# Turning three of eight blocks of z by a transposing DMA at their reload instead of on TensorE

## The chip, the cores and the metric

The kernel runs on one core of a Trainium2 chip, as one launch. The metric is the device time in microseconds (us). The engines are TensorE (PE), VectorE (DVE), ScalarE (ACT), GpSimd (POOL) and the DMA queues, which are fed here by SyncE (SP) and by POOL. On-chip memory has 128 partitions of SBUF and eight PSUM banks of 2 KB per partition.

## The reference

```python
mod = (silu(c) @ w_mod).reshape(1, 6, 1, 1024)
sa, ca, ga, sb, cb, gb = (mod[:, i] for i in range(6))
h = layernorm(x) * (1 + ca) + sa                    # x: 1 x 2048 x 1024
x = x + ga * (Cre @ (h @ Dre.T) - Cim @ (h @ Dim.T))  # DFT over hidden, then over sequence
h = layernorm(x) * (1 + cb) + sb
y = layernorm(h)
x = x + gb * (gelu(y @ w1 + b1) @ w2 + b2)          # w1: 1024 x 3584, w2: 3584 x 1024
```

All inputs and the output are 32-bit floats.

## The kernel before

**Arithmetic.** Every matrix product is made from 16-bit floats: an operand is split into a high half (the value rounded to 16 bits) and a low half (what is left), and three products high x high, high x low and low x high are added in PSUM (`PASSES`). Products are also blocked in the manner of Strassen and Winograd: two by two blocks need seven products instead of eight, so operands come as seven combinations `m` in the order `ORDER = (0, 1, 2, 4, 3, 6, 5)`, and results are added up from seven PSUM results. `right_tasks` makes the seven combinations of a right operand: its `hi` is an ACT copy to 16 bits (L386), its `comb` a DVE addition (L411), its `lo` a DVE subtraction (L396 without a scale, L398 with one).

**Stages.** First the modulation rows and the layer norm of x. Then the product over the sequence (`plain1`, `winograd1`, L1112 and L1162), whose result u goes through DRAM. Then the second product (`gemm2`, L1394), in eight blocks b of 256 rows: row r of 128 partitions takes pairs of tokens, `PIECES` lists its 14 pieces of 12 matmuls, each with a load of u (`load_up`, L1346). After block b come its residual, both layer norms and the modulation (`ln_tasks(b)`), in which 32-bit rows of z are left in `wb(b)` (two halves of 128 x 1024, written by the ACT instruction at L1279). `load_xw(b)` loads block b's x into the same place, of which there are two, so it waits for block b - 2 to be out of the way.

**The turn.** The MLP needs z with the hidden dimension on the partitions. `turn(b, n)` turns half n of block b: eight transposes of 128 x 128 on PE (`turn_tile`, L1296) into two PSUM banks, then an ACT copy to `zt(b, n)` (L1306). The function `turns`, called after each piece of `gemm2`, places them when the planner has the rows written: block k is turned in block k + 2 of `gemm2`, block 6 in part after its end and in part after the first pass of the MLP, block 7 after the third (`turn_late`, L1864). `z_tasks(b)` then splits the turned block into its seven combinations, high and low, and stores them with POOL's queue to DRAM (`zc_d`, L1328): four blocks to a half h of the tokens, h = 0 for blocks 0 to 3 and h = 1 for 4 to 7.

**The MLP.** `gemm3(g)` (L1585) makes 256 of the 3584 hidden units for half of the tokens: seven products of 12 matmuls, with w1 as the stationary operand and `zc(m)` in SBUF as the moving one. g = 0 to 13 take the first half of the tokens, 14 to 27 the second. Its results go through L1607 (ACT), L1611 (DVE) and L1604 (ACT, the gelu) and are split by `hid_tasks`. `gemm4(v)` (L1694) is the product with w2 and adds into `acc` (L1730, L1740). The order on PE is written out: gemm3(0), then for every v gemm3(2v+1), gemm3(2v+2), gemm4(v).

**The reload.** `zc(m)`, 1 MB each, is held once. The first half is loaded during the eighth block of `gemm2`, as the weights of the DFT in the same places come free. The second half is loaded during gemm3(13): after each of its products the hook `reload(m)` issues `load_zc(1, m)` on SP (L1336), and gemm3(14), which follows directly on PE, uses it one pass later.

**Order.** Work of DVE, ACT, POOL and the DMA queues is put into streams of tasks. A planner, which runs while the program is written and not on the chip, keeps a clock for each engine and picks from the streams by due time, estimated start and cost; what it picks becomes the fixed order of that engine's or queue's instructions. While `gemm2` is planned, DMAs are taken in the order of their estimated starts. `need(tag)` takes all tasks with a tag before going on. SP's queue is in order: an issue that waits for a semaphore holds up those behind it.

Of the kernel before, what the change touches and what calls it, by code (L numbers as in the profile page):

```python
# [10 lines left out]
F16 = mybir.dt.float16  # L11
# [6 lines left out]
P = 128  # L18
S = 2048
D = 1024  # L20
# [2 lines left out]
ND = D // P  # L23
TB = 512
NTB = S // TB
EPS = 1e-5


# [7 lines left out]
def kernel(ctx, tc, x, cre, cim, dre, dim, w1, b1, w2, b2, c, wm, out):  # L36
# [117 lines left out]
    O_K, O_ACC, O_HID = 32, 48, 172  # L154

    def zc(m):
        return at(O_ZC[m], 4096, F16).rearrange("p (a k c t) -> p a k c t", a=2, k=4, c=4)

    w1c = at(0, 14336, F16).rearrange("p (m s a x) -> p m s a x", m=7, s=2, a=2)
    w2c = at(144, 14336, F16).rearrange("p (m s a x) -> p m s a x", m=7, s=2, a=2)  # L160
# [13 lines left out]
    def quad(g):  # L174
# [2 lines left out]
    gb2_t = at(28, 1024)  # L177

    zc_d = [
        [dram.tile([P, 2, 4, 4, P], F16, tag=f"zc_{h}_{m}", name=f"zc_{h}_{m}") for m in range(7)] for h in range(2)  # L180
    ]
    s_d = {m: dram.tile([P, 8, 2, 512], F16, tag=f"s_{m}", name=f"s_{m}") for m in (2, 4, 3, 5)}
    u_d = [
        [[dram.tile([P, 2, 4, 2, P], F16, tag=f"u_{t}_{m}_{r}", name=f"u_{t}_{m}_{r}") for r in range(2)] for m in range(7)]
# [873 lines left out]


    PASSES = ((0, 0), (0, 1), (1, 0))  # L1060
    NB = NS // 2
    PIECES = [(m, ri) for m in ORDER for ri in range(2)]
    NP = len(PIECES)

# [139 lines left out]
    def ln_tasks(b):  # L1204

        y, w, cl = yb(b), wb(b), lns[b % 2]
        su, nm, v, ve, r, a = (cl[:, n, :] for n in range(6))
        junk = at(180, 1024, F16)

        def norm(src, scale):  # L1210
            def square(n):
# [64 lines left out]
        t.append(Task("dve", 0.16, lambda: dve.tensor_tensor(nm, nm, r, op=ALU.mult), [t[-1].key]))  # L1276
        k = t[-1].key
        for n in (1, 0):
            f = lambda n=n: act.activation(w[:, n], w[:, n], AF.Identity, scale=r[:, n : n + 1], bias=nm[:, n : n + 1])  # L1279
            t.append(Task("act", 1.25, f, [k], ("w", b, n)))  # L1280
        if b < NB - 1:
            n = len(two_)
# [5 lines left out]
        return t  # L1288

    def zt(b, n):  # L1290
        return at((O_K if b == NB - 1 else 144) + 4 * n, 1024)

    def turn_tile(b, n, ps):

# [3 lines left out]
    def turn(b, n):  # L1298
# [7 lines left out]
        f = lambda: act.activation(zt(b, n), ps, AF.Copy)  # L1306
        push("turn", f"turn{b}", [Task("act", 1.1, f, [("turn", b, n)], ("zt", b, n))], clk["pe"])

    def z_tasks(b):

        e, o = zt(b, 0), zt(b, 1)
        q = [e[:, 0:512], o[:, 0:512], e[:, 512:1024], o[:, 512:1024]]
        places = [O_K + 8 + 2 * k for k in range(4)] if b == NB - 1 else [152, 154, 46 if b == NB - 2 else 182, 216, 218]
        h, k = divmod(b, 4)
        n, at_ = [0], {}

        def outs(m):
            at_[m] = n[0]
            reuse("z", (b, n[0] - len(places)) if n[0] >= len(places) else None)
            if n[0] < len(places) and 0 < b < NB - 1:  # L1320
                need(f"z{b - 1}")
            v = at(places[n[0] % len(places)], 1024, F16).rearrange("p (a x) -> p a x", a=2)
            n[0] += 1
            return v[:, 0], v[:, 1], v

        def post(m, o_):
            dst = zc_d[h][m][:, :, k].rearrange("p a c t -> p a (c t)")
            store("z", (b, at_[m]), lambda: gp.dma_start(dst, o_[2]), ("z", b, m), f"z{b}")  # L1328

        return right_tasks(  # L1330
            q, outs, None, 512, lambda j: ("zt", b, j % 2), lambda m: ("z", b, m), post=post,
            free=lambda m: slot("z", lambda: (b, n[0] - len(places))),
        )

    def load_zc(h, m):
        sp.dma_start(at(O_ZC[m], 4096, F16), zc_d[h][m].rearrange("p a k c t -> p (a k c t)"))  # L1336

    def load_up(N):
        b, n = divmod(N, NP)
# [25 lines left out]
    def load_xw(b):  # L1365
        def f():
            need("st_u")
            sp.dma_start(wb(b), x[2 * b : 2 * b + 2].rearrange("r p e -> p r e"))

        was = [("turn", b - 2, n) for n in range(2)] if b > 1 else [("g1", opn(3, 5, 3))]  # L1370
        if b == 1:
            was += [("uw", 3, ri, m) for ri in range(2) for m in range(7)]
        return Task("dma", 3.0, f, was, ("xw", b))
# [150 lines left out]
        f = lambda q: lambda: sp.dma_start(raw2(0, q), w2[0:2, :, q, :].rearrange("j p x -> p j x"))  # L1524
        return [Task("dma", 1.5, f(q), [("w1", 2 - q // 2, m) for m in range(7)], ("raw2", 0, q)) for q in (2, 3, 0, 1)]

    waiting = deque((k, r) for k in range(NB - 1) for r in (1, 0))
    waiting.pop()

    def turns(b, n):  # L1530

        k, r = waiting[0] if waiting else (NB, 0)
        if k >= b:
            return
        last = NP - 1 if b == NB - 1 else 6 + 3 * (1 - r)
        keys = [("w", k, r)] + ([("zt", *((k, 1) if r == 0 else (k - 1, 0)))] if (k, r) != (0, 1) else [])
        zs = [("z", k - 1, m) for m in range(7)] if k and r else []
        while True:
            k, r = waiting[0]
            late = b == NB - 1 and n == NP - 1 or k < b - 1 and n >= last  # L1540
            if not late and any(done.get(x, 1e12) > clk["pe"] - 0.5 for x in keys + zs):
                return
            waiting.popleft()
            if r:
                need(f"z{k - 1}")
            turn(k, r)
            if r == 0:
                push("z", f"z{k}", z_tasks(k), clk["pe"] + 10.0)
            if not waiting or not late:
                return  # L1550

    def each(b):
        def f(n):
            turns(b, n)

            if n == 1 and 1 <= b < 4:
                push("wl", "wl", first_w1(b - 1))
                push("w", "w", w1_norm(b - 1) + w1_tasks(b - 1), clk["pe"] + 20.0)
            if n == 1 and b == 4:
                push("wl", "wl", first_w2())  # L1560
                push("w", "w", w2_norm(0) + w2_tasks(0), clk["pe"] + 60.0)
            if b == NB - 1:
                if n == 3:
                    need("w", "st_w1", *(f"z{k}" for k in range(4)))
                    for m in ORDER:
                        sp.dma_start(w1c[:, m, 0], w1_d[0][:, m])
                        done["w1", 0, m] = clk["pe"]
                if 4 <= n < 11:
                    load_zc(0, ORDER[n - 4])
                    m = ORDER[n - 4]  # L1570
                    sp.dma_start(w1c[:, m, 1], w1_d[1][:, m])
                    done["w1", 1, m] = clk["pe"]

        return f

    for b in range(NB):
        gemm2(b, each(b))
        push("ln", "ln", ln_tasks(b), clk["pe"] + 10.0)
    need("y")
    in_order[0] = False  # L1580

    def product3(ps, s, m, start):
        for d in range(4):
            for n, (a, b) in enumerate(PASSES):
                pe.matmul(  # L1585
                    ps.rearrange("p (k t) -> p k t", k=4),
                    w1c[:, m, s, a, d * P : (d + 1) * P],
                    zc(m)[:, b, :, d, :],
                    start=(start and d == 0 and n == 0),
                    stop=(d == 3 and n == 2),  # L1590
                    skip_group_check=not start,
                )
# [264 lines left out]

        return f

    def turn_late(b, n):  # L1860
        k, two = take(2)
        turn_tile(b, n, two)
        done["turn", b, n] = clk["pe"]
        act.activation(zt(b, n), two, AF.Copy)  # L1864
        done["zt", b, n] = clk["pe"] + 2.0
        leave(k, 2, clk["pe"] + 2.0)

    later[0] = True
    for j, k in enumerate((3, 4, 5, 6, 7, 1, 2, 0)):
        done["bank", k] = level() - 8.0 + j  # L1870
# [1 line left out]
    for kind, k in seq:  # L1872
        if kind == 3:
# [4 lines left out]
            if g == 0:  # L1878
# [1 line left out]
                    f = lambda m=m: sp.dma_start(w1c[:, m, 0], w1_d[2][:, m])  # L1880
                    Task("dma", 0.75, f, key=("w1", 2, m)).run()
                load_w1(3, *range(4))
                turn_late(NB - 2, 0)
                push("z", f"z{NB - 2}", z_tasks(NB - 2), due[3, 1] + 5)
                push("hid", "hid0", hid_tasks(0), due[3, 1] + 0)
            elif g == 1:
                need(f"z{NB - 2}", "ln", "st_w2", "st_x2")
                load_w1(4, 0, 1)
                for m in ORDER:
                    f = lambda m=m: sp.dma_start(w2c[:, m], w2_d[0][:, m])  # L1890
                    Task("dma", 1.5, f, key=("w2", 0, m)).run()
                push("hid", "hid1", hid_tasks(1), due[4, 0])
                push("w1", "n1_3", w1_norm(3), due[3, 3] - 20.0)
                push_w1(3)
            elif g == 2:
                turn_late(NB - 1, 1)
                turn_late(NB - 1, 0)
                push("z", f"z{NB - 1}", z_tasks(NB - 1), due[4, 0] + 10)
                push_w1(4)

                def f(q):
                    def load():
                        need(f"z{NB - 1}")
                        sp.dma_start(raw2(1, q), w2[2:4, :, q, :].rearrange("j p x -> p j x"))

                    return load

                was = [("z", NB - 1, m) for m in range(7)]
                push("w2", "l2_1", [Task("dma", 1.5, f(q), was, ("raw2", 1, q)) for q in range(4)], due[4, 1] - 20.0)
                push("w2", "n2_1", w2_norm(1), due[4, 1] - 20.0)  # L1910
            else:
                if g == 15:
                    need("fin")
                if g == 2 * NPAIR - 1:
                    push("hid", "hid27b", ht[0][:5], due[4, g // 2] - 20)
                    push("hid", "hid27c", ht[0][5:], due[4, g // 2] + 5)
                elif g % 2 == 1:
                    push("hid", f"hid{g}", hid_tasks(g), due[4, g // 2])
                push_w1(g + 2)
# [61 lines left out]
```

## Time and profile before

| | |
|---|---|
| median of 3 runs | 1991.37 us (1990.52 to 1992.13) |
| the profiled execution, first to last instruction (its span) | 1990.4 us |
| PE busy | 1969.1 us, 99% |
| DVE, ACT, POOL busy | 1417.3, 851.1, 190.5 us |
| mean granted TensorE clock | 0.999 |
| DMA traffic | 402.42 MB, mean 202 GB/s |
| PE transposes (L1296) | 128, 273 ns each, from 733.4 to 1021.1 us |
| stores of z (L1328) | 56 of 256 KB, 4.5 us to landing |
| loads of zc (L1336) | 14 of 1024 KB, 6.9 us to landing |

The profile is one execution seen by the hardware profiler; times in it are us from the span's start, durations of single instructions are ns. "Idle before" is the time for which an engine stood before an instruction, and the arrow names what ended it. SPq and POOLq are the queues that issue DMAs. Matmuls overlap: the row of a matmul lasts 379 ns, while consecutive ones start 216 ns apart.

### The profile page before, as it was taken

Reading aid. Unit: us, or ns where it says so; the run is one execution under the profiler, and the core shown is the slowest. Engines: PE = TensorE matmul, PEld = TensorE weight load, DVE = VectorE, ACT = ScalarE, POOL = GpSimd, SP = SyncE. Lnnn points to the kernel's source line nnn. Section 1 sums busy time; section 2 is a strip of 40 time slices with the busy share of each in tenths; the row PEclk is TensorE's granted clock in tenths of the full one; section 3 lists DMA queues with packets and bytes.
Section 4 is the critical chain, followed back from the end, with each engine's and each line's share of the span. In section 5 each row is a group of like instructions: output and inputs, shape, how many; then the busy total and the mean of one; then the engine's idle time right before and its main releaser. Section 6 shows DMA issues by size and latency. Waiting matters only on the chain. (4 is left out here: it accounts for less than half of the span.)

```text
span 1990.4 us, 23735 instructions
## 1 busy us (share of the span) xinstructions
PE 1969.1 (99%) x9082; PEld 896.5 (45%) x9082; DVE 1417.3 (71%) x1795; ACT 851.1 (43%) x1091; POOL 190.5 (10%) x282
## 2 busy tenths in 40 slices
PE   9999999999999999999999999999999999999999
PEld 3444444444444444444444444444444444444443
DVE  2977886997984467777588999999873353553566
ACT  2853432344542245554477566466233322312311
POOL 0002212221220112221020000000000000000000
PEclk9999999999999999999999999999999999999999
DMA  9138677678779777877765454453477332432323
GB/s 380 53 97 281 236 264 275 246 298 329 249 256 364 271 261 256 282 244 277 276 218 190 171 199 168 145 175 146 169 231 216 117 97 83 127 101 69 111 74 85
DMA packets 139363, 402.42 MB, mean 202 GB/s; under 512 B 15536, under 2 KB 15536, under 8 KB 134640
## 3 DMA queue, kind: packets, MB, share of 16 engines
q1 hardware_dynamic: 112528, 309.92, 45.3%
q0 software_dynamic: 26720, 90.98, 12.8%
q8 instruction: 71, 1.16, 0.2%
q14 instruction: 44, 0.36, 0.1%
HBM read 262.95 MB, written 137.89 MB: 201 GB/s over the span
## 5 line engine op out<-in xcount | busy, mean ns | idle before, releaser
L1694 PE MATMUL ps<-arena 128*128 128x512 f16 x2352 | 511.1, 379 | 2.8 <-DVE arena L1740 1.5
L1585 PE MATMUL ps<-arena 128*128 128x512 f16 x2352 | 510.2, 379 | 2.2 <-ACT arena L1607 2.2
L1162 PE MATMUL ps<-arena 128*128 128x512 f16 x2016 | 435.5, 379 | 1.4 <-DMA arena<-s 1.4
L1694 PEld LDWEIGHTS <-arena 128*128 128x128 f16 x2352 | 229.9, 98 | 281.5 <-issue 3.8
L1585 PEld LDWEIGHTS <-arena 128*128 128x128 f16 x2352 | 230.1, 98 | 279.4 <-issue 2.5
L1740 DVE SCALAR_TENSOR_TENSOR arena<-ps,i4c,arena 128x1024 f32<-128x1024 f32 x179 | 229.3, 1281 | 144.4 <-PE ps L1694 143.1
L1162 PEld LDWEIGHTS <-arena 128*128 128x128 f16 x2016 | 197.1, 98 | 239.5 <-DMA arena<-s 1.9
L1394 PE MATMUL ps<-arena 128*128 128x512 f16 x1344 | 292.4, 379 | 1.9 <-DMA arena<-u 1.9
L386 ACT ACTIVATE arena<-arena,shc 128x512 f16<-128x512 f32 (+1 forms) x115 | 115.9, 1018 | 277.3 <-PE ps L1694 184.6
L1394 PEld LDWEIGHTS <-arena 128*128 128x128 f16 x1344 | 131.4, 98 | 158.0 <-DMA arena<-u 2.4
L1112 PE MATMUL ps<-arena 128*128 128x512 f16 x768 | 167.4, 379 | 7.2 <-ACT arena L635 2.0
L411 DVE TENSOR_TENSOR arena<-arena 128x512 f32<-128x512 f32 (+1 forms) x228 | 171.0, 753 | 4.1
L681 ACT ACTIVATE arena<-arena 128x1024 f16<-128x1024 f32 x100 | 104.1, 1050 | 150.8 <-PE ps L1162 111.4
L398 DVE SCALAR_TENSOR_TENSOR arena<-arena,shc 128x512 f16<-128x512 f32 (+1 forms) x115 | 128.7, 1122 | 38.4 <-ACT arena L386 38.3
L684 DVE SCALAR_TENSOR_TENSOR arena<-arena 128x1024 f16<-128x1024 f32 x100 | 128.6, 1303 | 18.5 <-ACT arena L681 18.5
L1611 DVE TENSOR_TENSOR arena<-arena,ps 128x512 f32<-128x512 f32 x84 | 57.5, 685 | 110.7 <-PE ps L1585 106.5
L1604 ACT ACTIVATE arena<-arena,b1s,i1c 128x512 f32<-128x512 f32 x84 | 68.3, 813 | 137.0 <-DVE arena L1611 137.0
L1112 PEld LDWEIGHTS <-arena 128*128 128x128 f16 x768 | 74.7, 98 | 99.9 <-ACT arena L635 4.0
L773 ACT ACTIVATE arena<-arena 128x1024 f16<-128x1024 f32 x56 | 57.7, 1047 | 60.9 <-DVE arena L1186 18.8
L776 DVE TENSOR_TENSOR arena<-arena 128x1024 f16<-128x1024 f32 x56 | 66.9, 1218 | 14.6 <-ACT arena L773 14.6
L386 ACT ACTIVATE arena<-arena,s1c 128x512 f16<-128x512 f32 (+1 forms) x70 | 60.8, 884 | 36.9 <-DVE arena L411 25.9
L398 DVE SCALAR_TENSOR_TENSOR arena<-arena,s1c 128x512 f16<-128x512 f32 (+1 forms) x70 | 66.3, 959 | 11.0 <-ACT arena L386 10.8
(159 smaller groups left out, 1418.8 us busy)
## 6 DMA issues: line engine op xcount, KB each, us to landing
w<-arena SPq DMA_DIRECT2D x64, 512.0 KB, 5.0
arena<-w SPq DMA_DIRECT2D x119, 256.0 KB, 2.7
u<-arena POOLq DMA_DIRECT2D x56, 512.0 KB, 5.5
arena<-u SPq DMA_DIRECT2D x112, 256.0 KB, 4.0
arena<-w SPq DMA_DIRECT2D x56, 512.0 KB, 3.4
arena<-s SPq DMA_DIRECT2D x48, 512.0 KB, 7.6
arena<-in_cre_dram SPq DMA_DIRECT2D x32, 512.0 KB, 7.3
arena<-in_cim_dram SPq DMA_DIRECT2D x32, 512.0 KB, 5.2
```

Source lines behind the costliest of these rows:

```text
L386: act.activation(o[m][0], q(j), AF.Copy, **sc)
L398: dve.scalar_tensor_tensor(o[m][1], q(j), scale, o[m][0], op0=ALU.mult, op1=ALU.subtract)
L411: dve.tensor_tensor(q(d), q(a), q(b), op=op)
L681: h = Task("act", 1.15, lambda: act.activation(o[:, :, 0], s2, AF.Copy, scale=SC), list(deps) + free)
L684: dve.scalar_tensor_tensor(o[:, :, 1], s2, SC, o[:, :, 0], op0=ALU.mult, op1=ALU.subtract)
L1112: pe.matmul(bank_of(d_), hleft(d_, s, kp, a), cop(n)[:, s, b], start=(kp == 0 and s == 0 and a == 0 and b == 0), stop=(kp == 7 and s == 1 ...
L1162: pe.matmul(bank_of(st + ch), left, cop(n)[:, s, b], start=(start and kp == 0 and s == 0 and a == 0 and b == 0), stop=(kp == 3 and s == 1 ...
L1394: pe.matmul(bank_of(bk), up(N)[:, c_, a], dp(n)[:, c_, w], start=(start and ri == 0 and c_ == 0 and i == 0), stop=(ri == 1 and c_ == 3 and ...
L1585: pe.matmul(ps.rearrange("p (k t) -> p k t", k=4), w1c[:, m, s, a, d * P : (d + 1) * P], zc(m)[:, b, :, d, :], start=(start and d == 0 and ...
L1604: act.activation(dst, src, AF.Gelu_apprx_tanh, scale=inv, bias=b1s[:, 2 * p + j : 2 * p + j + 1])
L1694: pe.matmul(t[:, j], hidc[:, c_, m, a, k * P : (k + 1) * P], w2c[:, m, c_, w], start=(start and c_ == 0 and n == 0), stop=(c_ == 1 and n = ...
L1740: lambda: dve.scalar_tensor_tensor(dst, ps[b], inv, dst, op0=ALU.mult, op1=ALU.add), kp[b],
```

## The change

Blocks 0 to 4 are turned on PE as before (`TURNED = 5`). Blocks 5, 6 and 7 aren't: `z_tasks` splits their rows as they stand, token on the partition, and stores the seven combinations to new tensors `zl_d[m]` (128 x 3 x 1024, 16 bits). `load_zc(1, m)` becomes two DMAs on SP: a transposing one of 128 x 3072 elements from `zl_d[m]`, 24 blocks of 128 x 128, and a plain one of block 4's 128 x 1024. For that the layout of `zc` becomes block by block, so that the stores of z write one run of 2 KB per partition in place of two of 1 KB. `turn_late` and its four calls go; the split of blocks 5 and 6 is pushed during `gemm2`, once blocks 0 to 4 are turned (`later_z`), and the split of block 7 where its turns stood. `load_xw(7)` waits for the splits of block 5, which now read `wb(5)`. Block 7's rows are written to `O_K` (`zw`), and some scratch places move.

```diff
@@ constants
+NB = NS // 2
+TURNED = 5
@@ places and DRAM tensors
     def zc(m):
-        return at(O_ZC[m], 4096, F16).rearrange("p (a k c t) -> p a k c t", a=2, k=4, c=4)
+        return at(O_ZC[m], 4096, F16).rearrange("p (k a c t) -> p k a c t", k=4, a=2, c=4)
...
     zc_d = [
-        [dram.tile([P, 2, 4, 4, P], F16, tag=f"zc_{h}_{m}", name=f"zc_{h}_{m}") for m in range(7)] for h in range(2)
+        [dram.tile([P, 4 * (1 - h) + (TURNED - 4) * h, D], F16, tag=f"zc_{h}_{m}", name=f"zc_{h}_{m}") for m in range(7)]
+        for h in range(2)
     ]
+    zl_d = [dram.tile([P, NB - TURNED, D], F16, tag=f"zl_{m}", name=f"zl_{m}") for m in range(7)]
@@ ln_tasks
-        junk = at(180, 1024, F16)
+        junk = at(O_K + 8 if b == NB - 1 else 180, 1024, F16)
...
-            f = lambda n=n: act.activation(w[:, n], w[:, n], AF.Identity, scale=r[:, n : n + 1], bias=nm[:, n : n + 1])
+            f = lambda n=n: act.activation(zw(b)[:, n], w[:, n], AF.Identity, scale=r[:, n : n + 1], bias=nm[:, n : n + 1])
@@ zt, zw and z_tasks
     def zt(b, n):
-        return at((O_K if b == NB - 1 else 144) + 4 * n, 1024)
+        return at(144 + 4 * n, 1024)
...
+    def zw(b):
+        return at(O_K, 2048).rearrange("p (r e) -> p r e", r=2) if b == NB - 1 else wb(b)
...
-        e, o = zt(b, 0), zt(b, 1)
+        e, o = (zw(b)[:, n] if b >= TURNED else zt(b, n) for n in range(2))
+        src = "w" if b >= TURNED else "zt"
...
-        places = [O_K + 8 + 2 * k for k in range(4)] if b == NB - 1 else [152, 154, 46 if b == NB - 2 else 182, 216, 218]
+        if b < TURNED:
+            places = [152, 154, 182, 216, 218]
+        else:
+            places = [O_K + 8 + 2 * k for k in range(4)] if b == NB - 1 else [144 + 2 * k for k in range(6)]
...
-            dst = zc_d[h][m][:, :, k].rearrange("p a c t -> p a (c t)")
-            store("z", (b, at_[m]), lambda: gp.dma_start(dst, o_[2]), ("z", b, m), f"z{b}")
+            dst = zc_d[h][m][:, k] if b < TURNED else zl_d[m][:, b - TURNED]
+            v = o_[2].rearrange("p a x -> p (a x)")
+            store("z", (b, at_[m]), lambda: gp.dma_start(dst, v), ("z", b, m), f"z{b}")
...
-            q, outs, None, 512, lambda j: ("zt", b, j % 2), lambda m: ("z", b, m), post=post,
+            q, outs, None, 512, lambda j: (src, b, j % 2), lambda m: ("z", b, m), post=post,
@@ load_zc
-        sp.dma_start(at(O_ZC[m], 4096, F16), zc_d[h][m].rearrange("p a k c t -> p (a k c t)"))
+        n = 4 if h == 0 else TURNED - 4
+        o = at(O_ZC[m], 4096, F16)
+        if h:
+            v = o[:, n * D :].rearrange("p (n t) -> p n t", t=P)
+            sp.dma_start_transpose(v, zl_d[m].rearrange("p k x -> p (k x)"))
+        if n:
+            sp.dma_start(o[:, 0 : n * D], zc_d[h][m].rearrange("p k x -> p (k x)"))
@@ load_xw
-        was = [("turn", b - 2, n) for n in range(2)] if b > 1 else [("g1", opn(3, 5, 3))]
+        was = [("g1", opn(3, 5, 3))]
+        if b > 1:
+            was = [("turn", b - 2, n) for n in range(2)] if b - 2 < TURNED else [("z", b - 2, m) for m in range(7)]
@@ turns during gemm2
-    waiting = deque((k, r) for k in range(NB - 1) for r in (1, 0))
-    waiting.pop()
+    waiting = deque((k, r) for k in range(TURNED) for r in (1, 0))
+    later_z = deque()
...
-        last = NP - 1 if b == NB - 1 else 6 + 3 * (1 - r)
+        last = 6 + 3 * (1 - r)
...
-            late = b == NB - 1 and n == NP - 1 or k < b - 1 and n >= last
+            late = k < b - 1 and n >= last
...
             turns(b, n)
+            while later_z and not waiting:
+                k, t = later_z.popleft()
+                push("z", f"z{k}", z_tasks(k), t)
...
         gemm2(b, each(b))
-        push("ln", "ln", ln_tasks(b), clk["pe"] + 10.0)
+        push("ln", f"ln{b}", ln_tasks(b), clk["pe"] + 10.0)
+        if TURNED <= b < NB - 1:
+            later_z.append((b, clk["pe"] + 40.0))
@@ product3
-                    zc(m)[:, b, :, d, :],
+                    zc(m)[:, :, b, d, :],
@@ the order of the MLP (turn_late removed)
-                turn_late(NB - 2, 0)
-                push("z", f"z{NB - 2}", z_tasks(NB - 2), due[3, 1] + 5)
+                need(f"ln{NB - 2}")
                 push("hid", "hid0", hid_tasks(0), due[3, 1] + 0)
             elif g == 1:
-                need(f"z{NB - 2}", "ln", "st_w2", "st_x2")
+                need(f"z{NB - 2}", f"ln{NB - 1}", "st_w2", "st_x2")
...
             elif g == 2:
-                turn_late(NB - 1, 1)
-                turn_late(NB - 1, 0)
                 push("z", f"z{NB - 1}", z_tasks(NB - 1), due[4, 0] + 10)
```

More of the change, by code (lines that the diff above doesn't have):

```diff
@@ L1060 @@
     PASSES = ((0, 0), (0, 1), (1, 0))
-    NB = NS // 2
     PIECES = [(m, ri) for m in ORDER for ri in range(2)]
@@ L1858, in hook @@
         return f
[L1860 to L1866, printed above, removed]
     later[0] = True
```

## The prediction

> **What bounds the kernel now.** I read the page's head first, then the waits of TensorE (PE), then the timeline of PE around the removed instructions.
>
> ```profile
> span 1990.4 us, 23735 instructions
> PE 1969.1 (99%) x9082; PEld 896.5 (45%) x9082; DVE 1417.3 (71%) x1795; ACT 851.1 (43%) x1091; POOL 190.5 (10%) x282
> ...
> PE ps L1585 <- ACT arena L1607: 2.2, 1, 2.2
> ...
> PE ps L1394 <- DMA arena<-u: 1.9, 1, 1.9
> ```
>
> PE is busy 1969.1 of 1990.4 us, and its waits are a handful of single events. Nothing else is near: VectorE (DVE) 71%, ScalarE (ACT) 43%. So an instruction taken off PE shortens the run by the time by which it moves the next matmul, as long as nothing new makes PE wait. Two of the waits lie in the region that the change rearranges. The rows of PE there (start, length, engine and line, operation, count, idle before and what ended it):
>
> ```profile
> 926.06 1.04 PE L1296 MATMUL ps<-ident,arena 128*128 128x128 f32 x8
> 926.94 5.34 PE L1394 MATMUL ps<-arena 128*128 128x512 f16 x24
> 932.12 1.04 PE L1296 MATMUL ps<-ident,arena 128*128 128x128 f32 x8
> 932.99 23.47 PE L1394 MATMUL ps<-arena 128*128 128x512 f16 x108
> 958.38 2.76 PE L1394 MATMUL ps<-arena 128*128 128x512 f16 x12 [1.92 <-DMA arena<-u]
> 960.98 1.04 PE L1296 MATMUL ps<-ident,arena 128*128 128x128 f32 x8
> 961.86 18.29 PE L1585 MATMUL ps<-arena 128*128 128x512 f16 x84
> 979.99 1.04 PE L1296 MATMUL ps<-ident,arena 128*128 128x128 f32 x8
> 980.86 23.47 PE L1585 MATMUL ps<-arena 128*128 128x512 f16 x108
> 1006.54 13.11 PE L1585 MATMUL ps<-arena 128*128 128x512 f16 x60 [2.21 <-ACT arena L1607]
> 1019.49 1.91 PE L1296 MATMUL ps<-ident,arena 128*128 128x128 f32 x16
> 1021.23 5.34 PE L1694 MATMUL ps<-arena 128*128 128x512 f16 x24
> ```
>
> The L1296 rows are the turns of blocks 5, 6 and 7: six halves of eight transposes.
>
> **Part 1, the turns leave PE: -5.2 us.** What a turn costs the path is the distance from its start to the next matmul's start, since matmuls overlap. 926.94-926.06 = 0.88, 932.99-932.12 = 0.87, 961.86-960.98 = 0.88, 980.86-979.99 = 0.87, and 1021.23-1019.49 = 1.74 for the last two: 5.24 us for 48 transposes, 0.109 us each, and no idle time in front of any of them. All of it is on the path. The duration in the row below, 0.273 us, would give 13.1, but it covers pipeline time in which neighbours run.
>
> ```profile
> L1296 PE MATMUL ps<-ident,arena x128: 272/273/273, 733.4 to 1021.1; 128*128 128x128 f32 x128
> L1306 ACT ACTIVATE arena<-ps x13: 1023/1023/1024, 734.5 to 962.1; 128x1024 f32<-128x1024 f32 x13
> ```
>
> The Trainium skill (TensorE: Matmul & The Clock Gate, Part 4: PE-mode transpose) gives about 275 ns for a transpose in one kernel's context; the row's 273 ns agrees as a duration, but charged 48 times it would put the gain at 13.2 us, and the start-to-start distances say 5.24.
>
> The six PSUM copies that go with the turns (1.02 us each on ACT, three at L1306 and three at L1864) go too: 6.1 us of an engine at 43%. They count only where ACT makes PE wait, which is part 2.
>
> **Part 2, the splits of blocks 5 and 6 come earlier: about -1.5 us.** The splits are unchanged in size (seven L386 of 0.63 us on ACT, L396 and L411 of 0.69 us on DVE, seven stores on POOL); they only stop waiting for a turn. Block 6 now runs here:
>
> ```profile
> 1004.11 1.89 ACT L386 ACTIVATE arena<-arena 128x512 f16<-128x512 f32 x3 [0.78 <-DVE arena L411]
> 1005.91 0.58 ACT L1607 ACTIVATE arena<-ps 128x512 f32<-128x512 f32 x1
> ...
> 961.00:984.00 23.00, 23.00 (x116) 11.43 (x115) 12.60 (x29) 12.47 (x17) 0.00 (x0) 1.00 0.75 277
> 984.00:1007.00 23.00, 20.79 (x98) 9.33 (x96) 18.05 (x38) 16.30 (x24) 4.50 (x8) 1.00 0.33 121
> ```
>
> The three unscaled L386 at 1004.11 belong to block 6. The PSUM copy L1607 that PE waits for stands behind them and starts at 1005.91; PE resumes at 1006.54. In the window rows (length, PE, weight loads, DVE, ACT, POOL) ACT has 16.3 of 23 us in 984 to 1007 and 12.5 in 961 to 984. The new code pushes block 6's split while the eighth block of the second product is still running, so it should be over before 985 and the three L386 are gone from the queue. Ends: the full 2.21 back, or nothing, if the same 0.63-us pieces get in the way of an eviction elsewhere (one such collision costs 0.6). I take 1.5, nearer the first, because the earlier window has ACT and DVE half free. Block 7 keeps its place; without its turns it is at most 1 us earlier, and I count nothing.
>
> **Part 3, the load of x for block 7 now waits for block 5's split instead of its turn: about -1.0 us.** In the queue of SP, with the time to landing of those two loads of u and the windows' row under them:
>
> ```profile
> 936.66 0.39 SPq L1368 DMA_DIRECT2D arena<-in_x_dram  x1
> ...
> 939.22 0.44 SPq L1346 DMA_DIRECT2D arena<-u  x1
> ...
> 942.00 0.54 SPq L1346 DMA_DIRECT2D arena<-u  x1
> ...
> DMA to landing us min/median/max: 14.0/15.2/16.3
> ...
> 935.00:961.00 26.00, 24.08 (x113) 10.79 (x112) 18.71 (x43) 9.56 (x16) 5.97 (x9) 1.00 0.95 369
> ```
>
> The last two loads of u take 14.0 and 16.3 us to land, because the DMA engines are 95% busy (369 GB/s) with block 7's x (1 MB), the first half of zc and the weights; the second lands at 958.3, and PE resumes at 958.38. All of this is released by PE, so it moves up together by the 1.75 us of the two turns before it. What changes is the x load. Block 5's split could start when its normalised rows are written, at 921.0:
>
> ```profile
> 918.65 2.37 ACT L1279 ACTIVATE arena<-arena,lns 128x1024 f32<-128x1024 f32 x2 [2.05 <-DVE lns L1276]
> ...
> 934.25 1.15 ACT L386 ACTIVATE arena<-arena 128x512 f16<-128x512 f32 x2
> ...
> 956.21 2.13 POOL L1328 DMA_DIRECT2D zc<-arena  x3 [4.83 <-DVE arena L396]
> ```
>
> Before, the split ran from 934.3 to the issue of its last stores at 958.3, 24 us; started at 921 it ends near 945, and the x load can go then. If its place in SP's queue is behind the two u loads, they have 1 MB less ahead of them: 1.049 MB at 369 GB/s = 2.8 us, more than the wait of 1.92. If it stands ahead of them, the zc loads, weights and u loads queue behind it: the last u load goes at 945 instead of 940.2, lands 14.0 to 16.3 us later at 959.0 to 961.3, and is needed where PE ran dry before (932.99+23.47 = 956.46) less 1.75, at 954.7: a wait of 4.3 to 6.6, so 2.4 to 4.7 us lost. The queue is written by estimated start time, which favours the first order. Ends -1.9 and +4.7; I take -1.0, half of the first end. Block 7's normalisation, which needs this x, may start some us later; PE no longer waits for it at all, and its split is pushed only where the two turns at 1019.49 stood.
>
> The stores of z become 2 KB per partition instead of two pieces of 1 KB; POOL is at 10% and nothing on the path waits for them: nothing.
>
> **Part 4, the transposing load: 0.** One 1-MB load per product becomes 768 KB transposed and 256 KB plain. The place:
>
> ```profile
> 1422.96 36.42 PE L1585 MATMUL ps<-arena 128*128 128x512 f16 x168
> 1459.22 1.03 PE L1694 MATMUL ps<-arena 128*128 128x512 f16 x4
> ...
> 1425.74 8.09 SPq L1336 DMA_DIRECT2D arena<-zc  x4
> 1433.94 0.37 SPq L1050 DMA_DIRECT2D w<-arena  x1
> 1436.11 5.50 SPq L1336 DMA_DIRECT2D arena<-zc  x3
> ...
> 1461.48 3.74 SPq L1018 DMA_DIRECT2D arena<-w  x7
> ...
> GB/s 0 0 0 9 151 416 425 372 425 425 337 434 399 283 381 266 310 434 452 425 425 425 425 425 434 407 394 401 401 412 399 390 419 290 248 354 22 0 0 0
> ...
> DMA to landing us min/median/max: 4.8/5.9/7.0
> ...
> 1423.00:1441.00 18.00, 18.00 (x85) 8.20 (x84) 16.98 (x17) 6.42 (x8) 0.00 (x0) 1.00 0.79 294
> ```
>
> The 168 matmuls are two passes of seven products; each product is 12 matmuls, 36.26/14 = 2.59 us. Load k (0 to 6) is released at 1425.74+2.59k and needed by the second pass, which starts at 1422.96+18.1, at 1441.1+2.59k, so the last is needed at 1456.6: 30.9 us for all seven. Of these go 2.3 of latency (4.8 landing less 1.049 MB at 425 GB/s, the level that most slices of the stretch 1423 to 1460 hold in the row above), 1.2 for the 512-KB store between them, and seven plain parts of 0.62: 4.3. That leaves 23.1, or T = 3.3 us for each transposed part (238 GB/s). Below it PE waits for nothing; above it PE loses 7 x (T-3.3).
>
> No transposing transfer stands in the trace, so T is bounded: from below by the plain rate, 0.786 MB at 425 GB/s = 1.85 us; from above by letting each 256-byte run of a 128x128 block cost as much as the queue's average packet.
>
> ```profile
> q1 hardware_dynamic: 112528, 309.92, 45.3%
> ```
>
> That packet took 0.453 x 16 x 1990.4/112528 = 0.128 us; 24 blocks of 128 runs over 16 engines are 192 packets, 24.6 us. I take the row nearest in place and kind, the 294 GB/s that this stretch moved: 2.7 us, under the 3.3, so nothing is lost. Behind the transposes SP's queue holds stores and weight loads; the passes that use those weights start after the 168 matmuls from 1459.22, at 1495.5, 34 us after the second group of L1018 begins, so some 5 us of delay cost nothing.
>
> The Trainium skill (DMA: Bandwidth & Descriptors, Latency and other measured facts) gives 261 GB/s for a DMA transpose: an estimate of 3.0 us, again no loss, though only 2 us in all are then left.
>
> **Sum.** -5.24 -1.5 -1.0 +0 = -7.7 us. The profiled span, 1990.4, lies 1.0 below the median of 1991.37; 1991.4-7.7 = 1983.6, with 1982.7 for a span.
>
> **Rivals.** (a) Only the turns count: parts 2 and 3 give waits back as large as they remove. 1991.4-5.2 = 1986.1. For it: two waits of 2 us that end on different engines; against: ACT and DVE have room where the work goes. (b) The x load stands ahead of the u loads in SP's queue, and PE's wait near 957 grows to 5.4 us: -5.2-1.5+3.5 = -3.2, 1988.2, inside 0.2% (4 us), which is about what a measurement can tell from no change. (c) The other side: the transposing loads are slow, and PE waits in the second pass at 1441 to 1459, L1585 on a DMA from zl. With parts 1 to 3 worth 7.7, no change is at T = 3.3+7.7/7 = 4.4 us (179 GB/s) and slower by 4 us at T = 5.0 (157 GB/s). At the upper bound of 24.6 us it is 7 x 21.3 = 149-7.7: 2133 us. For it: this stretch is nearly full already, so there is no second cover; against: seven plain loads there leave 9 us over. A page of the Trainium skill speaks for it (VectorE: DVE Perf Modes, The three transpose paths): 1309 ns for a 128x128 block by DMA, which one after the other would be an estimate of 31 us a load and some 195 us lost; no run here shows whether blocks follow one another so. (d) The turns don't leave the path: excluded, since no idle time lies before them.
>
> **How the numbers follow.** As forecast 0.50, (a) 0.20, (b) 0.12, (c) 0.18, of which I count 0.15 slower by over 0.2% and 0.03 within it. So faster 0.70, same 0.15, slower 0.15. Low end: 5.24+2.21+1.92 and the smaller ACT waits of 0.75 in this region gone: 1981.2. High end: through (b) and the mild part of (c), 1992; the rest of (c), about 0.15, stays outside. The forecast's own range is 1981.2 to 1987.
>
> **What would show it.** L1296 with 80 instead of 128 instructions and PE busy down by about 13 us of overlapping durations; no row of PE waiting for L1607 near 1000; the wait on u below 1.9 us; on SP seven transposing issues from about 1418 and none of the L1585 products in the second pass waiting for zl. The prediction is wrong if a transposed load takes over 4 us, or if the waits on u or on ACT grow.

## The result, and the profile after

The changed kernel takes 2000.78 us (median of 4 runs, 1999.98 to 2002.15) against 1991.28 before (4 runs): 1.0049 of the time, 95% interval 1.0035 to 1.0064. It is slower by 0.49%, outside the predicted range of 1981.2 to 1992.0. The profiled execution took 1999.98 us, the lowest of the four, with a span of 1998.2, 7.8 us above the profiled span before; the traces below explain these 7.8, and the rest up to the medians' 9.5 is spread between executions.

Lines of the new file are shifted: the products of the MLP are L1611 and L1720 (before L1585 and L1694), the second product L1414, the turn L1299, the PSUM copies that PE waits for L1633 and L1756 (before L1607 and L1730). The page's head and PE's waits (line, what it waited for, us in total, times, longest):

```profile
span 1998.2 us, 23631 instructions
PE 1966.7 (98%) x9034; PEld 891.3 (45%) x9034; DVE 1417.6 (71%) x1795; ACT 845.8 (42%) x1085; POOL 180.5 (9%) x282
...
PE ps L1611 <- ACT arena L1633: 5.5, 1, 5.5
PE ps L1720 <- ACT arena L1756: 4.7, 2, 3.8
PE ps L1611 <- DMA arena<-zc: 4.2, 3, 1.9
PE ps L1720 <- DVE arena L1766: 2.4, 2, 1.8
```

PE has the 48 instructions less. The wait on u is gone, both waits for ACT have grown, and one on zc is new. Where they lie, from PE's timeline:

```profile
896.79 59.73 PE L1414 MATMUL ps<-arena 128*128 128x512 f16 x276
956.36 41.60 PE L1611 MATMUL ps<-arena 128*128 128x512 f16 x192
1003.42 14.88 PE L1611 MATMUL ps<-arena 128*128 128x512 f16 x60 [5.46 <-ACT arena L1633]
...
1047.69 2.75 PE L1720 MATMUL ps<-arena 128*128 128x512 f16 x12 [0.90 <-ACT arena L1756]
1054.28 7.03 PE L1720 MATMUL ps<-arena 128*128 128x512 f16 x24 [3.84 <-ACT arena L1756]
1061.14 36.42 PE L1611 MATMUL ps<-arena 128*128 128x512 f16 x168
...
1456.10 2.75 PE L1611 MATMUL ps<-arena 128*128 128x512 f16 x12 [1.02 <-DMA arena<-zc]
1460.80 2.75 PE L1611 MATMUL ps<-arena 128*128 128x512 f16 x12 [1.95 <-DMA arena<-zc]
1464.81 2.75 PE L1611 MATMUL ps<-arena 128*128 128x512 f16 x12 [1.26 <-DMA arena<-zc]
```

In the kernel before, the same stretch ends so:

```profile
1026.80 26.06 PE L1694 MATMUL ps<-arena 128*128 128x512 f16 x120 [0.22 <-ACT arena L1730]
1053.39 5.34 PE L1694 MATMUL ps<-arena 128*128 128x512 f16 x24 [0.53 <-ACT arena L1730]
1058.56 36.42 PE L1585 MATMUL ps<-arena 128*128 128x512 f16 x168
```

At 956.36 the MLP starts 5.5 us earlier than before (961.86): the wait on u and half of the turns are saved by then. At 1061.14 the fourth pass starts 2.6 us later than before (1058.56): 8.1 us went in 105 us, and since the other 2.6 us of turns were saved in the same stretch, 10.7 us were lost in it. The reload takes another 4.2.

The balance in us, against the profiled execution before: turns -5.24; wait on u -1.92; waits for ACT 5.46+0.90+3.84 against 2.21+0.22+0.53, +7.24; the matmuls behind the two long ones, 60 in 14.88 against 13.11 and 24 in 7.03 against 5.34, +3.46; zc +4.23; a wait of L1720 on DVE 2.4 against 1.5, +0.9; and -0.78, by which this execution reached the second product earlier in code that the change doesn't touch. Sum +7.9; the spans differ by 7.8. Two small terms are left out and nearly cancel: each wait moves the next matmul by 0.16 us more than its length (there are two more waits now, +0.33), and the time from the last matmul to the end of the span is 0.38 shorter.

**The wait of 5.5 us.** ACT's queue in the changed kernel:

```profile
992.82 0.78 ACT L1630 ACTIVATE arena<-ps,b1s,i1c 128x512 f32<-128x512 f32 x1
993.50 1.14 ACT L1215 ACTIVATE arena<-arena,lns 128x1024 f16<-128x1024 f32 x1
...
994.76 1.15 ACT L1215 ACTIVATE arena<-arena,lns 128x1024 f16<-128x1024 f32 x1
...
998.87 2.37 ACT L1282 ACTIVATE arena<-arena,lns 128x1024 f32<-128x1024 f32 x2 [2.26 <-DVE lns L1279]
...
1002.79 0.58 ACT L1633 ACTIVATE arena<-ps 128x512 f32<-128x512 f32 x1
```

PE ran dry at 956.36+41.60 = 997.96. L1633, the copy that frees its bank, stands last. Ahead of it is the end of block 7's normalisation: two sums of squares (L1215), 2.26 us of idling for the small DVE steps that turn them into a scale, and the two rows of z (L1282). Before, the sums of squares stood a pass earlier relative to PE:

```profile
985.18 1.14 ACT L1212 ACTIVATE arena<-arena,lns 128x1024 f16<-128x1024 f32 x1
...
987.74 1.13 ACT L1212 ACTIVATE arena<-arena,lns 128x1024 f16<-128x1024 f32 x1
```

In the changed kernel neither their data nor a busy ACT sets their time:

```profile
989.62 0.17 DVE L1218 TENSOR_SCALAR lns<-lns 128x2 f32<-128x2 f32 x1
...
991.02 0.81 ACT L1630 ACTIVATE arena<-arena,b1s,i1c 128x512 f32<-128x512 f32 x1 [1.78 <-DVE arena L1637]
```

Their last operand (L1218) is written by 989.8 and ACT stands idle until 991.02, but they start at 993.50, behind that gelu and two more instructions. DVE's part of the chain had stood behind L1637, the addition for PE's products, in the same way, with 2.24 us of idling before 987.70.

**The waits of 0.9 and 3.8 us.** SP's queue and ACT's:

```profile
1036.85 8.87 SPq L1919 DMA_DIRECT2D arena<-in_w_dram  x4
1045.83 0.41 SPq L878 DMA_DIRECT2D arena<-in_w_dram  x1
...
1052.08 1.03 ACT L899 ACTIVATE ps<-arena 128x1024 f32<-128x1024 f32 x1 [4.44 <-issue]
...
1053.13 1.09 ACT L1756 ACTIVATE arena<-ps,i4c 128x1024 f32<-128x1024 f32 x1
```

The four loads of w2 pair 1 (L1919) take 8.87 us to issue. Their places are those from which block 7's z is being stored, and 6.1 us of that time is one wait of SP for a store to zl. The load of w1 group 4 (L878) stands behind them and lands 6.2 us after its issue at 1045.83, at 1052.0; the sum of squares that reads it (L899) starts at 1052.08, after ACT stood idle for 4.44 us, and L1756 for PE stands behind that. The row of L899 names no releaser ("issue"), so that it waited for this load is read from the times; e2 tests it.

### The profile page after: what moved, and what is told of

It reads as the page before. It is cut to its first block, busy times and chain, and to the rows that moved or that the text cites. A ratio compares the mean times of both kernels' runs of the same rounds, so it can differ in the third digit from the quotient of the medians.

```text
span 1998.2 us, 23631 instructions
## 1 busy us (share of the span) xinstructions
PE 1966.7 (98%) x9034; PEld 891.3 (45%) x9034; DVE 1417.6 (71%) x1795; ACT 845.8 (42%) x1085; POOL 180.5 (9%) x282
## 3 DMA queue, kind: packets, MB, share of 16 engines
q1 hardware_dynamic: 134256, 309.92, 46.6%
q0 software_dynamic: 26720, 90.98, 12.7%
## 4 chain that ended last, share of the span: by engine, by line
PE 76%; DVE 12%; DMA 6%; issue 3%; ACT 2%; POOL 0%; SPq 0%; DVEq 0%; ACTq 0%; POOLq 0%
PE ps L1720 22%; PE ps L1611 22%; PE ps L1414 15%; PE ps L1165 13%; DMA s<-arena 2%; DVE arena L688 2%; DMA arena<-in_wm_dram 2%; PE ps L478 1%; DVE arena L402 1%; DVE arena L720 1%; DVE arena L637 1%; DVE arena L638 1%; DMA arena<-s 1%; DVE arena L780 1%; DVE arena L792 1%
## 5 line engine op out<-in xcount | busy, mean ns | idle before, releaser
L1611 PE MATMUL ps<-arena 128*128 128x512 f16 x2352 | 512.3, 380 | 9.7 <-ACT arena L1633 5.5
L1720 PE MATMUL ps<-arena 128*128 128x512 f16 x2352 | 512.8, 380 | 7.7 <-ACT arena L1756 4.7
L1611 PEld LDWEIGHTS <-arena 128*128 128x128 f16 x2352 | 230.3, 98 | 289.5 <-issue 13.8
L1720 PEld LDWEIGHTS <-arena 128*128 128x128 f16 x2352 | 230.3, 98 | 287.9 <-issue 11.0
L1414 PE MATMUL ps<-arena 128*128 128x512 f16 x1344 | 291.9, 379 | 0.0
L1414 PEld LDWEIGHTS <-arena 128*128 128x128 f16 x1344 | 131.5, 98 | 156.4
L1637 DVE TENSOR_TENSOR arena<-arena,ps 128x512 f32<-128x512 f32 x84 | 57.5, 685 | 110.8 <-PE ps L1611 105.6
L1633 ACT ACTIVATE arena<-ps 128x512 f32<-128x512 f32 x84 | 49.7, 592 | 60.2 <-PE ps L1611 60.2
```

The lines of the kernel that those rows point to most:

```text
L1414: pe.matmul(bank_of(bk), up(N)[:, c_, a], dp(n)[:, c_, w], start=(start and ri == 0 and c_ == 0 and i == 0), stop=(ri == 1 and c_ == 3 and ...
L1611: pe.matmul(ps.rearrange("p (k t) -> p k t", k=4), w1c[:, m, s, a, d * P : (d + 1) * P], zc(m)[:, :, b, d, :], start=(start and d == 0 and ...
L1720: pe.matmul(t[:, j], hidc[:, c_, m, a, k * P : (k + 1) * P], w2c[:, m, c_, w], start=(start and c_ == 0 and n == 0), stop=(c_ == 1 and n = ...
```

## The experiments

The theory: the transposing load costs the 4.2 us that its waits show, and the rest is order. Block 6's split, free of its turn, is given to the planner with an earlier due time than block 7's normalisation, and the queues written from that have work that isn't ready ahead of the copies that PE needs. Rivals: the stretch of DMA is full whatever the loads; ACT and DVE have too much to do; block 7's x is late. Differences to the changed kernel are between medians that were taken beside different runs of the kernel before; they hold to a microsecond or two.

### e1: plain loads in place of the transposing ones

```diff
-            sp.dma_start_transpose(v, zl_d[m].rearrange("p k x -> p (k x)"))
+            sp.dma_start(o[:, n * D :], zl_d[m].rearrange("p k x -> p (k x)"))
```

> The changed kernel with its seven transposing loads replaced by plain loads of the same 768 KB; nothing else moves. Blocks 5 to 7 reach the second half of the MLP unturned, so this leaves the turn out of the computation. The changed kernel waits 4.2 us for zc in its second pass of the reload. Theory A (the transposing load costs what those three waits show): 4.2 us come back, about 1996.5 us, and no wait of L1611 on zc. Rival B (the loads queue as long when plain, because this stretch of DMA is full of stores and weights): under 1 us comes back, about 2000. In both, the waits for ACT near 1003 and 1054 us stay.

1996.4 us (10 runs), 1.0023 of before (1.0014 to 1.0033): 4.4 under the changed kernel (5.2 by the ratios to the kernel before). PE's timeline over both passes of the reload, without a wait:

```profile
1424.69 36.42 PE L1611 MATMUL ps<-arena 128*128 128x512 f16 x168
```

The waits for ACT stay at 5.47, 0.93 and 3.70. So rival B falls, the transposing costs about 4 us, and the larger loss is not in it. How long PE waits in the reload differs between executions, though: 4.2 us in the changed kernel, and 3.3, 2.7 and 4.0 in e2, e3 and e10, which leave the reload as it is.

### e2: the loads of w2 pair 1 behind those of w1 group 4

```diff
-                was = [("z", NB - 1, m) for m in range(7)]
+                was = [("z", NB - 1, m) for m in range(7)] + [("raw1", 4, k) for k in (2, 3)]
```

> The changed kernel, with the four loads of w2 pair 1 put behind the loads of w1 group 4 in SP's queue. Theory A (they wait there for block 7's stores of z, and hold up the w1 loads behind them, so that ACT stands in a norm and the PSUM copies behind it are late): the waits of 3.8 and 0.9 us at 1047 to 1054 and the 1.7 us of slow clock after them go, 6.4 us, about 1994.4. Rival B (ACT is late there because it has too much to do): no change, about 2000.8. The wait of 5.5 us at 1003 stays in both.

1994.48 us (10 runs), 1.0013 of before (1.0004 to 1.0023): 6.3 back of 6.4 expected, which is closer than the parts are. One wait of 1.3 is left of 0.9 and 3.8, and from the start of the MLP to its fourth pass the profiled execution is 4.8 us shorter than the changed kernel's; the rest lies elsewhere, 0.9 of it in the reload's waits:

```profile
1004.50 15.27 PE L1611 MATMUL ps<-arena 128*128 128x512 f16 x60 [5.46 <-ACT arena L1633]
...
1049.56 7.99 PE L1720 MATMUL ps<-arena 128*128 128x512 f16 x36 [1.30 <-ACT arena L1756]
```

### e3: block 7's x early

```diff
-        return at(O_W + 8 * (b % 2), 2048).rearrange("p (r e) -> p r e", r=2)
+        return at(192 if b == 7 else O_W + 8 * (b % 2), 2048).rearrange("p (r e) -> p r e", r=2)
...
-            was = ... if b - 2 < TURNED else [("z", b - 2, m) for m in range(7)]
+            was = ... if b < NB - 1 else [("w2", 0, m) for m in range(7)]
```

> The changed kernel with block 7's x loaded into a place of its own (192 KB up), so that it no longer waits for block 5's split. Theory A (block 7's normalisation is late because its x is late, and its last steps stand in ACT's queue in front of the copy L1633 that PE waits for at 1003): the normalisation ends 4 us or more earlier, the wait of 5.5 us and the 1.8 us of slow clock after it go mostly, about 1994 us. Rival B (it is late because block 6's split now stands ahead of it in the queues of ACT and DVE): the wait shrinks by less than 2 us, about 1999 to 2001.

2000.88 us (4 runs), 1.0046 (1.0031 to 1.0061), and the same wait of 5.46. The load is issued at 899.7, 43 us earlier, and ACT's order up to the fourth pass is the same to the instruction; so is the end of the normalisation, with the first sum of squares at 993.16 and L1633 at 1002.46.

Its theory A fell: a late x was not the cause, though DVE does wait 1.85 us for it in the changed kernel. With the same order the chain ends at the same time. That the total is the same is in part chance: the later wait for L1756 is 5.70 here instead of 3.84, and the waits on zc are 2.7 instead of 4.2.

### e4: six blocks turned

```diff
-TURNED = 5
+TURNED = 6
```

> The changed kernel with six blocks turned on TensorE and two left to the transposing load (512 KB transposed and 512 KB plain per product). Block 5's x-load wait is as in the kernel before. Theory A (the loss comes from the order at the start of the MLP and from the transposed bytes): two turns cost 1.75 us again, the reload's wait of 4.2 falls to 0 to 1 us, and the waits for ACT change with the order; between 1990 and 1998 us. Rival B (any transposing load costs a fixed time): the wait in the reload stays near 4 us.

2002.23 us (5 runs, 1997.81 to 2005.82), 1.0048 (1.0032 to 1.0064): above the expected range. The wait of 5.46 for ACT is there too, with 0.84 and 2.98 later, and that on u is back (1.84). The profiled execution is the lowest of the five, so no trace shows what made the others slower. The wait on zc is 2.0, between the two theories and under the 2.7 to 4.2 of the runs with the whole reload; how much of it goes with the bytes can't be told from one execution. On SP the seven loads of 512 KB still hold the queue for 3.1 to 4.3 us each but the first (2.05); those of 768 KB hold it for 3.13 to 5.96.

### e6: block 6's split due 30 us later

```diff
-            later_z.append((b, clk["pe"] + 40.0))
+            later_z.append((b, clk["pe"] + (40.0 if b < NB - 2 else 70.0)))
```

> The changed kernel with one number changed: block 6's split is due 70 us after the end of its block of the second product, not 40, so that the planner puts block 7's normalisation ahead of it. In the program written with it ACT's copies for the third pass of the MLP no longer stand behind the end of that normalisation, and the loads of w1 group 4 no longer behind those of w2 pair 1. Theory A (the two waits for ACT come from the order that the earlier split led the planner to): the 5.5 us wait shrinks to 2 us or less and the pair of 0.9 and 3.8 goes, with the slow clock after them, 10 us or more in all, about 1990. Rival B (ACT has more to do there than it can): PE loses about as much at other places, 1998 to 2001. The reload's 4.2 us stays in both.

1985.35 us (5 runs), 0.9966 of before (0.9954 to 0.9978): 15.4 us under the changed kernel by one number, and faster than the kernel before.

```profile
955.66 41.60 PE L1611 MATMUL ps<-arena 128*128 128x512 f16 x192
999.14 13.11 PE L1611 MATMUL ps<-arena 128*128 128x512 f16 x60 [1.88 <-ACT arena L1633]
...
1048.43 36.42 PE L1611 MATMUL ps<-arena 128*128 128x512 f16 x168
...
1441.39 2.75 PE L1611 MATMUL ps<-arena 128*128 128x512 f16 x12 [1.06 <-DMA arena<-zc]
1445.77 2.75 PE L1611 MATMUL ps<-arena 128*128 128x512 f16 x12 [1.63 <-ACT arena L1630]
1449.61 2.75 PE L1611 MATMUL ps<-arena 128*128 128x512 f16 x12 [1.09 <-DMA arena<-zc]
```

The fourth pass starts at 1048.43, 12.7 us earlier than in the changed kernel, 12.0 of them won since the start of the MLP. ACT and DVE have the same work to do as in the changed kernel, so the rival that they have too much falls. The two sums of squares stand inside the second pass in ACT's queue:

```profile
980.67 1.13 ACT L1215 ACTIVATE arena<-arena,lns 128x1024 f16<-128x1024 f32 x1
...
982.28 1.14 ACT L1215 ACTIVATE arena<-arena,lns 128x1024 f16<-128x1024 f32 x1
```

In SP's queue both loads of w1 group 4 stand ahead of those of w2 pair 1 now (1020.02 and 1027.90 against 1030.33), so the same number took away the cause of the waits of 0.9 and 3.8 too. The waits of L1720 on DVE fall from 2.4 to 0.2. In the reload 2.2 us of waits on zc are left and one of 1.63 for ACT, whose cause wasn't followed. The reason for the number: block 7's normalisation is due 10 us after the end of the eighth block, which is 36.3+10 = 46.3 us after the end of the seventh, and the split was due at 40. No run tells whether the order flips just there.

### e8: the plain loads on POOL's queue

```diff
-            sp.dma_start(o[:, 0 : n * D], zc_d[h][m].rearrange("p k x -> p (k x)"))
+            (gp if h else sp).dma_start(o[:, 0 : n * D], zc_d[h][m].rearrange("p k x -> p (k x)"))
```

> The changed kernel with the seven plain loads of block 4 issued by POOL's queue, so that the transposing loads follow one another on SP; all other orders are the same. Theory A (a transposing load moves its bytes in 2.7 us, but each next one is issued only after the last is nearly over and a plain load besides, and needs another 1 us to begin): the period between transposing loads falls from 4.2 to 4.8 us to about 3.3, and the wait of 4.2 us goes to 1 or less, about 1997. Rival B (the DMA engines are full in this stretch, and the order of the loads doesn't matter): the wait stays at 3 to 4 us, about 2000.

1997.9 us (5 runs), 1.0039 (1.0025 to 1.0054): 2.9 back. The reload's waits fall from 4.2 to 1.6. SP's queue now holds only transposing loads there:

```profile
1428.41 18.71 SPq L1352 DMA_TRANSPOSE arena<-zl  x4
...
1447.86 11.34 SPq L1352 DMA_TRANSPOSE arena<-zl  x3
```

Four take 4.7 us each while plain loads run beside them, three 3.8. The expected 3.3 wasn't reached; the difference between the four and the three fits that the plain loads now take on the DMA engines part of what they no longer take on SP, but no run shows it apart.

### e9: both, and e2's edit with them

> Both edits: block 6's split due at 70 us, and the plain loads on POOL's queue. If the causes are the two told of and independent, both gains add up: PE keeps the 5.2 us of the turns and the 1.9 of the wait on u, and the waits for ACT and zc fall to what the kernel before had or less, about 1985 to 1987 us, faster than the kernel before by 0.2 to 0.3%. If the waits only move, it stays at 1990 or above.

1983.01 us (5 runs), 0.9957 of before (0.9945 to 0.9970). The kernel has a third edit that the expectation doesn't name: the line of e2, by which the loads of w2 pair 1 wait for those of w1 group 4. They stand in that order in e6 without it, and ACT's order from 940 to 1130 us is e6's to the instruction, so it is not seen to change anything; but e9 is not a test of two edits alone. The gains of e6 and e8, 15.4 and 2.9, add up to within a microsecond of the 17.8 here. Against e6 alone the median is 2.3 us lower, with intervals that overlap. One wait of 0.51 on zl is left in the reload, one of 1.87 for ACT at the third pass, and one of 0.70 for L1756.

### e10: the demand for block 7's normalisation later

```diff
@@ before the third pass of the MLP
-                need(f"z{NB - 2}", f"ln{NB - 1}", "st_w2", "st_x2")
...
-                for m in ORDER: (loads of w2, v = 0)
@@ after the third product of that pass
+        need(f"z{NB - 2}", f"ln{NB - 1}", "st_w2", "st_x2")
+        for i in ORDER: (the same loads)
```

> The changed kernel, block 6's split as early as in it, but the demand that block 7's normalisation and the other work be written out (need, with the loads of w2 behind it) moved from before the third pass of the MLP to after that pass's third product, so that the end of the normalisation needn't stand in ACT's queue ahead of that pass's first copies. Theory A (the 5.5 us wait is made by this demand, which puts a chain that isn't ready in front of L1633): the wait falls below 2 us, and the time to 1993 or less, the more so as the order of the norm's squares behind it changes too. Rival B (the early split itself leaves ACT and DVE no room): PE waits as long for the second or third copy, 1998 or more. The reload's 4 us stay.

1993.68 us (10 runs), 1.0005 (0.9995 to 1.0015), between the two theories: 7.1 back, but the wait didn't fall below 2.

```profile
954.73 46.78 PE L1611 MATMUL ps<-arena 128*128 128x512 f16 x216
1005.16 9.33 PE L1611 MATMUL ps<-arena 128*128 128x512 f16 x36 [3.65 <-ACT arena L1633]
...
1046.61 10.78 PE L1720 MATMUL ps<-arena 128*128 128x512 f16 x36 [3.63 <-ACT arena L1756]
```

PE gets two products further, and then waits for a copy behind the same L1282. So the demand sets the place of this wait; that the normalisation's lateness sets most of its size fits with e6, which takes both away. The second wait, 3.63, has again a sum of squares (L899) ahead of it that stands for 5.36 us until a weight load lands. In the profiles only 2.3 us of the gain lie between the start of the MLP and its fourth pass, and 2.4 are the waits of L1720 on DVE, which are gone.

## Why the prediction was wrong

**Part 1** held: -5.24 us, and PE's row of 276 matmuls from 896.79 runs through where two turns stood. One of its signs was misread: PE's busy time counts overlapping instructions once (9082 of them, most of 379 ns, make 1969 us), so it could not fall by 13 us; it fell by 2.4, the turns less the slower matmuls. **Part 3** held in sign and mechanism, and the whole 1.92 came back instead of 1.0. On SP x went behind the last load of u:

```profile
941.16 0.32 SPq L1364 DMA_DIRECT2D arena<-u  x1
...
942.96 0.38 SPq L1386 DMA_DIRECT2D arena<-in_x_dram  x1
```

In e4, where x waits for a turn again and is issued at 933.51, ahead of the last two loads of u, the wait on u is back at 1.84.

**Part 2** is the step that failed. It took the earlier split as work moved into free time: -1.5 us, with an upper end of nothing. The runs showed +7.24 of waits for ACT and +3.46 of slow clock behind them, 10.7 us. The argument looked at how busy ACT and DVE are (half) and not at order. Block 6's split did leave the place where it had delayed L1607, as forecast. But the waiting instruction was looked for only behind the split itself; it stood behind what the split displaced, block 7's normalisation, which a demand then forced in ahead of the third pass. e6 gives the part its predicted sign: with the split due later, the waits for ACT up to the fourth pass go from 2.96 before to 1.88, -1.1 where -1.5 was predicted. Rival (a), a loss as large as the gain there, named no such mechanism. Block 7, of which the prediction said that PE no longer waits for it at all, was the one that PE waited for: its turn was gone, its place in ACT's queue was not.

**Part 4** failed too: it had the right quantity, the time of a transposing load, and missed a term. The rate inside a transposing load, by half-microsecond slices of 1429 to 1449:

```profile
GB/s 0 0 0 110 161 286 291 290 289 178 66 389 283 235 289 290 290 295 181 274 231 52 18 285 291 289 291 280 201 292 225 180 281 289 291 246 48 238 385 426
```

Inside the load it holds at 290, which makes 0.786 MB/290 = 2.7 us, as the prediction took T. But the start and the end are slower: the first load's bytes take the seven slices from 1430.5 to 1434 (0.80 MB), nearer 3.5 us than 2.7. Between loads stands a dip of a microsecond, and the issues show why:

```profile
1429.21 3.13 SPq L1352 DMA_TRANSPOSE arena<-zl  x1
1432.39 0.57 SPq L1354 DMA_DIRECT2D arena<-zc  x1
1433.06 3.44 SPq L1352 DMA_TRANSPOSE arena<-zl  x1
...
1446.70 5.96 SPq L1352 DMA_TRANSPOSE arena<-zl  x1
...
1453.71 3.67 SPq L1352 DMA_TRANSPOSE arena<-zl  x1
```

A plain issue holds SP for 0.57 or 0.58 us here (0.32 to 0.74 in e1), a transposing one for 3.13 to 5.96. So the next one comes when the last is nearly over, and its first bytes over a microsecond after that (issued at 1429.21, first bytes after 1430.5). The seven come 3.85 to 7.0 us apart instead of T plus plain, 3.3 us; the longest, 1446.70 to 1453.71, is the one behind the store of w at 1446.21. The threshold of 3.3 us for T held no such gap, and PE lost 4.23 us where 0 was forecast. The 261 GB/s that the prediction cites from the Trainium skill (DMA: Bandwidth & Descriptors, Latency and other measured facts), which the page gives for a transfer with a non-contiguous middle dimension, lies between the 290 inside a load and what the loads reach together: seven of 0.786 MB from the issue at 1429.2 to the wait's end at 1464.8, 155 GB/s, beside the plain parts and a store. The 1309 ns for a block of 128x128 in the Trainium skill (VectorE: DVE Perf Modes, The three transpose paths) did not add up block by block: 24 blocks take some 3.5 us, not 31.

Rival (c) was the right side, but not for its reason: by its price the kernel gets slower by 4 us only at a T of 5.0, and the reload alone leaves the kernel faster, as e6 shows with 2.2 us of waits on zc and 1.63 for ACT in it.

## What to carry to other kernels

Where a planner writes the queues, price a moved step by what it is put ahead of, by due times, and look for what that displaced work stands in front of; busy shares don't show it. An edit that takes work off the bounding engine should be judged after its neighbours' due times are set again: here one number made +0.49% into -0.34%. Price a chain of transposing DMAs by the distance between their issues, not by bytes over rate.

## What the runs showed of the hardware

A transposing load of 768 KB of 16-bit elements moves at 290 GB/s inside and holds its queue for 3.13 us or more. The queue carried 134256 packets instead of 112528: 21728 more, or 3104 for each of the seven loads, of which 24 x 128 = 3072 are as many as there are 256-byte runs in its blocks. An estimate from 2.7 us for 192 of them on each of 16 engines is 14 ns each, not the 128 that served as the upper bound.

PE's clock falls after most long waits. The windows (length, PE, weight loads, DVE, ACT, POOL, granted clock, DMA share, GB/s) after the wait of 5.46, after that of 3.84, and, in e1, after one of 3.70:

```profile
1003.40:1008.00 4.60, 4.58 (x14) 1.71 (x13) 2.68 (x3) 1.85 (x2) 0.00 (x0) 0.60 0.92 309
1054.20:1058.00 3.80, 3.72 (x11) 1.32 (x11) 2.83 (x7) 3.77 (x8) 0.00 (x0) 0.58 0.07 25
```

```profile
1054.30:1058.00 3.70, 3.67 (x18) 1.66 (x18) 2.73 (x7) 3.70 (x6) 0.00 (x0) 1.00 0.04 15
```

A wait of 5.46 or 5.47 us cost 1.3 to 2.8 us more in this way (60 matmuls in 14.39 to 15.90 against 13.11), and waits of 3.6 to 3.8 cost 1.3 to 2.8 or nothing. The Trainium skill (TensorE: Matmul & The Clock Gate, Part 1: The HAM clock gate) tells of a free-running activity window of about 3.4 us, one idle one of which halves the clock. These rows agree with it: a gap little longer than a window may or may not hold a whole one. One row doesn't fit a window that is idle throughout: in e3 two waits of 0.45 and 2.26, with 12 matmuls between them, were followed by 24 matmuls in 7.03 us instead of 5.34, while one of 2.98 in e4 cost nothing:

```profile
1461.99 7.03 PE L1611 MATMUL ps<-arena 128*128 128x512 f16 x24 [2.26 <-DMA arena<-zc]
```

So in the MLP of these runs a wait of 3.6 us or more on PE cost its length and, in all cases but one, 1.3 to 2.8 us besides.
